# A new order for the first 28 slices of an attention-and-feed-forward kernel: eight PSUM banks for products before the first output tile, fewer fillers

## The chip, the core and the metric

The kernel runs on one core of a Trainium2 chip. The metric is the device time of one launch in microseconds (us), as the median of several executions. The kernel before takes about 224.4 us. The work is almost all on TensorE, so this is a case about the last half per cent: what a hand-laid or computed order of instructions can still win or lose in the first 57 us.

## The reference, cut to what matters

```python
def _attn_ref(x, state):                     # x: (8, 8, 512, 64), state: (8, 8, 32, 64)
    scores = scale * x @ state^T             # 512 x 32 for each batch and head
    a = softmax(scores);  xread = a @ state
    a2 = softmax(scale * state @ x^T);  sread = a2 @ x
    return concatenate([xread, sread], axis=2)

def reference(x, state, w_gate, w_val, w_out):
    y = attn(x, state) reshaped to (8*544, 512)
    return (relu(y @ w_gate) * (y @ w_val)) @ w_out      # 512 -> 1536 -> 512
```

Inputs and output are float32; the kernel computes in bf16 with float32 sums.

## The kernel before

For the x rows, the product `a @ state @ w` is reordered: first `U = state @ w` for each batch (small products, "c" and "u" units), then `a @ U` ("gv" slices of 128 of the 1536 columns, four matmuls of 128x512 each), then relu and multiply, then the output product ("o" parts). The state rows are read by small "sr" products. The kernel uses eight banks of PSUM, the memory that the products are written to, and names the bank of each tile by a number. The first 28 gv slices, with all preparation, are laid out by hand in a list of words; later slices are generated by a loop.

```python
    def bank(name, kind="r"):
        if given:
            n = given.pop(0)                 # the listed program: the number after @
        ...
        else:
            n = turn["r"] % 6 if kind == "r" else 6 + turn["o"] % 2      # the generated part
            turn[kind] += 1
        return psum.tile([128, 512], FP32, name=name, tag=f"b{n}")

    def u_mm(dst, b, w, lo, n):              # U units: 64x32 tiles of the array, in groups of eight
        for j in range(NJ):
            for parity in range(2):
                r = 64 * parity
                nc.tensor.matmul(dst[parity][32 * j:32 * j + 32], stT[r:r + 64, b, j, ...],
                                 wsb[r:r + 64, j, lo:lo + n], start=True, stop=True)

    def gv_mm(ps, b, jf, w, kc):             # full products, 128x128 weights, 512 columns
        nc.tensor.matmul(ps[w], U[b][:, w, kc, f0:f0 + 128], ANS[b][:, kc]..., ...)

    def sr_mm(b, kind="r"):                  # 32 small products into one bank
        ps = held["sr", b] = bank("sr_ps", kind)[:, 0:2 * DP]...
    def sr_norm(b):                          # VectorE reads that bank: reciprocal, then multiply
        nc.vector.reciprocal(out=rr, in_=ps[:, :, D])
        nc.vector.tensor_tensor(out=sn, in0=ps[:, :, 0:D], in1=rr..., op=ALU.mult)

    def spin(n, cols=512):                   # fillers: products on zeros, to keep the array busy
        for i in range(n):
            nc.tensor.matmul(warm_ps[:, 0:cols], warm[:, 0:128], warm[:, 0:cols], ...)

    program = """
    dx.1.0.2 ... spin.7 stT.0@0 xc.0.0.dve dw.0.0.128 sto.0.act ...
    [... some 240 words: loads (dw, dx), transposes (xT, aT), scores (sc), U units (c, u) and
         their copies (co, uo), slices (gv, re, mu), output parts (o) ...]
    gv.2.0@21 mu.1.8 re.2.0 o.0.7 mu.2.0 o.0.8 o.0.9@7 of.0.2.dve sr.1@3 sn.1 xp.2 xp.3
    """
    [... then a loop: gv, relu, mult for slices 28 to 107, with o parts and the next batches]
```

Read `c.1.512.256@54` as: U unit of batch 1, columns 512 to 767, in banks 5 and 4. `sr.1@3` is the sr product of batch 1 in bank 3.

The softmax here doesn't subtract the row's maximum and nothing guards it: scores larger than these inputs give would overflow.

Of the kernel before, what the change touches and what calls it, by code (L numbers as in the profile page):

```python
# [16 lines left out]
def kernel(  # L17
# [52 lines left out]
    stT = const.tile([128, B, NJ, 64], BF16, name="stT")  # L70
# [5 lines left out]
    xf, xb, xT, e_sn, a_sn, ANS, U, hsb, sr_sb = {}, {}, {}, {}, {}, {}, {}, {}, {}  # L76
# [362 lines left out]
             "c": c_unit, "co": c_out, "u": u_unit, "uo": u_out, "gv": gv, "re": relu, "mu": mult, "o": out_part,  # L439
             "of": fin_x, "xn": x_next, "xp": x_pad, "sr": sr_mm, "sn": sr_norm}  # L440
    program = """
    dx.1.0.2 dx.1.1.2 stc.0.0.act stc.0.1.dve spin.7 stT.0@0 xc.0.0.dve dw.0.0.128 sto.0.act dw.1.0.128 on xc.0.1.dve
    spin.3 xT.0.1@1 dw.0.128.128 xT.0.0@2 xo.0.1.dve xo.0.0.act dw.1.128.128 spin.3 sc.0.0@3 dw.0.256.256 ex.0.0
    spin.1 xT.0.2@4 xT.0.3@5 xo.0.2.dve dw.1.256.256 xo.0.3.act nr.0.0 spin.3 sc.0.1@0 dw.0.512.256 xT2.1.0@1 ex.0.1
    nx.0.0 xo2.1.0.act nr.0.1 dw.1.512.256 spin.2 xT2.1.1@2 xo2.1.1.act sc.1.0@3 dw.0.768.256 nx.0.1 ex.1.0
    dw.1.768.256 spin.2 c.1.0.128@45 c.0.0.128@01 co.1.0.128.0.dve aT.0.1@2 co.0.0.128.0.act aT.0.0@3 co.1.0.128.1.dve
    co.0.0.128.1.act dw.0.1024.256 sc.1.1@4 ao.0.1.dve ao.0.0.act nr.1.0 ex.1.1 dw.1.1024.256 spin.2 c.0.128.128@05
    gv.0.0@12 co.0.128.128.1.act nr.1.1 co.0.128.128.0.act nx.1.0.pool re.0.0 gv.0.1@34 mu.0.0 re.0.1 nx.1.1.pool
    c.1.128.128@50 mu.0.1 co.1.128.128.1.act c.0.256.256@12 co.1.128.128.0.act c.1.256.256@30 dw.0.1280.256
    co.0.256.256.0.dve co.0.256.256.1.act aT.1.1@5 aT.1.0@4 co.1.256.256.0.act co.1.256.256.1.dve dw.1.1280.256  # L450
    gv.0.3@21 ao.1.1.act ao.1.0.dve dx.2.0.1 re.0.3 gv.0.2@30 mu.0.3 ds re.0.2 c.1.512.256@54 mu.0.2 gv.1.2@21
    co.1.512.256.1.act co.1.512.256.0.act do.0.6 c.0.512.256@30 re.1.2 gv.1.5@45 co.0.512.256.0.dve xp.1
    co.0.512.256.1.act mu.1.2 re.1.5 gv.1.3@23 mu.1.5 re.1.3 gv.1.1@04 do.6.12 mu.1.3 re.1.1 c.1.768.256@15 xp.0
    mu.1.1 gv.1.4@23 co.1.768.256.0.act co.1.768.256.1.act c.0.768.256@04 re.1.4 gv.1.0@15 co.0.768.256.0.dve
    co.0.768.256.1.act df.3 mu.1.4 re.1.0 gv.1.6@20 mu.1.0 re.1.6 gv.0.4@41 mu.1.6 re.0.4 gv.0.6@35 mu.0.4 re.0.6
    gv.1.7@20 mu.0.6 re.1.7 c.0.1024.256@41 c.0.1280.256@35 mu.1.7 co.0.1024.256.0.act xT2.2.0@2 stc.1.0.pool
    co.0.1024.256.1.act co.0.1280.256.1.dve xT2.2.1@0 stc.1.1.pool co.0.1280.256.0.act xo2.2.0.dve gv.0.5@41
    stc.3.0.pool stc.3.1.pool xo2.2.1.dve re.0.5 stc.2.1.pool gv.0.10@53 stc.2.0.pool mu.0.5 re.0.10 stT.1@2 gv.0.9@40
    mu.0.10 sto.1.act re.0.9 sc.2.1@1 gv.0.8@52 ex.2.1 mu.0.9 re.0.8 nr.2.1 gv.0.11@34 re.0.11 mu.0.8 gv.0.7@10
    nx.2.1.pool mu.0.11 re.0.7 sc.2.0@5 o.0.0@6 mu.0.7 ex.2.0 nr.2.0 c.1.1280.256@32 c.1.1024.256@14  # L460
    co.1.1280.256.1.act u.2.1.1024@50 o.0.1 co.1.1024.256.0.dve co.1.1024.256.1.act nx.2.0.pool uo.2.1.1024.1.dve
    uo.2.1.1024.0.act o.0.2 co.1.1280.256.0.act u.2.0.0@21 xn.3 of.0.0.dve u.2.1.0@45 uo.2.0.0.1.act u.2.1.512@03
    uo.2.1.0.0.dve o.0.3@7 uo.2.1.0.1.act uo.2.0.0.0.dve uo.2.1.512.0.act aT.2.0@1 aT.2.1@4 uo.2.1.512.1.dve
    ao.2.0.act o.0.4 ao.2.1.act o.0.5 gv.2.1@50 of.0.1.act re.2.1 gv.1.10@23 mu.2.1 re.1.10 gv.1.11@14 mu.1.10 re.1.11
    gv.2.3@50 mu.1.11 re.2.3 gv.2.2@23 mu.2.3 re.2.2 u.2.0.1024@14 u.2.0.512@50 mu.2.2 uo.2.0.1024.1.act sr.0@2
    o.0.6@6 uo.2.0.512.1.act uo.2.0.512.0.dve sn.0 gv.1.9@34 uo.2.0.1024.0.dve re.1.9 gv.1.8@05 mu.1.9 re.1.8
    gv.2.0@21 mu.1.8 re.2.0 o.0.7 mu.2.0 o.0.8 o.0.9@7 of.0.2.dve sr.1@3 sn.1 xp.2 xp.3
    """
    for word in program.split():
        word, _, banks = word.partition("@")  # L470
# [107 lines left out]
```

## Time and profile before

| | before |
|---|---|
| time, median of 3 | 224.46 us (224.29 to 224.59) |
| execution that was profiled | 225.65 us, span on the core 223.9 us |
| TensorE (PE) busy | 96% of the span |
| first gv product | 14.43 us |
| first generated slice (slice 28) | 57.28 us |

The profiled execution is 1.2 us longer than the median of the timed ones.

In the views PE is TensorE, DVE is VectorE, ACT is ScalarE and POOL is GpSimd. The page of the profile, its lines for the span, for PE, and the rows of busy tenths for PE and the loads (40 slices of 5.6 us; 9 is 90% or more; the DMA row counts packet time over 16 engines; its 0 in the eighth place is 7%, with 24 GB/s moved there), and the chain that ended last, by engine:

```profile
span 223.9 us, 4840 instructions
...
PE 215.5 (96%) x1937; PEld 105.8 (47%) x1967; DVE 129.0 (58%) x226; ACT 124.8 (56%) x236; POOL 53.0 (24%) x58
...
PE   7899999999999999999999999999999999999994
...
DMA  7999999070146671781159114511311111111132
...
PE 84%; DMA 9%; POOL 4%; issue 2%; DVE 0%; POOLq 0%; DVEq 0%
```

PE is the limit. The loads are full from the second to the seventh slice, to 39 us, so the listed program meets the load queue there; no later slice reaches 90%.

The timeline of PE in the kernel before, 16.9 to 25 us (columns: start us, length us, engine, line, operation, out<-in, shape, count, and idle time before it if any):

```profile
16.86 0.30 PE L291 MATMUL upc<-wv_sb,stT 64*32 64x256 bf16 x8
...
17.44 0.62 PE L235 MATMUL aT_ps<-id,a_sn 128*128 128x128 bf16 x8
17.97 1.90 PE L316 MATMUL gv_ps<-ans,U 128*128 128x512 bf16 x7
19.80 0.30 PE L291 MATMUL upc<-wg_sb,stT 64*32 64x256 bf16 x8
19.92 0.29 PE L291 MATMUL upc<-wv_sb,stT 64*32 64x256 bf16 x8
20.15 1.04 PE L316 MATMUL gv_ps<-ans,U 128*128 128x512 bf16 x4
21.11 0.30 PE L291 MATMUL upc<-wg_sb,stT 64*32 64x256 bf16 x8
21.23 0.29 PE L291 MATMUL upc<-wv_sb,stT 64*32 64x256 bf16 x8
21.46 2.77 PE L316 MATMUL gv_ps<-ans,U 128*128 128x512 bf16 x11
24.15 0.30 PE L291 MATMUL upc<-wg_sb,stT 64*32 64x256 bf16 x8
24.27 0.29 PE L291 MATMUL upc<-wv_sb,stT 64*32 64x256 bf16 x8
24.50 1.04 PE L316 MATMUL gv_ps<-ans,U 128*128 128x512 bf16 x4
```

No idle time is printed, because a matmul's modelled end (0.38 us after its start) hides gaps shorter than that. The starts tell more. Four products of a gv slice start 0.216 us apart, so a slice is worth 0.86 us; but from 20.15 to 21.11 us, one slice, are 0.96 us, and a single unit between slices takes 0.35 us (19.80 to 20.15), although its second half starts 0.12 us after its first. So TensorE loses time in going from full products to 64x32 tiles and back. (Some matmul records are missing from a trace, hence counts like x7 and x11.)

And the end of the listed program in the kernel before, same columns:

```profile
55.10 1.89 PE L353 MATMUL o_ps<-wo_sb,h_sb 128*128 128x512 bf16 x8
56.92 0.43 PE L264 MATMUL sr_ps<-xa,e_sn 128*32 128x65 bf16 x32
57.28 1.04 PE L316 MATMUL gv_ps<-ans,U 128*128 128x512 bf16 x3
```

The slice at 57.28 us is the first generated one; the last of the 32 sr products starts at 57.16 us, so the gap between the two is 0.13 us.

### The profile page before, as it was taken

What the parts mean: (1) busy time and instruction counts of PE and PEld (TensorE: products, weight loads), DVE (VectorE), ACT (ScalarE), POOL (GpSimd) and SP (SyncE); (2) the same over time, 40 slices, a digit from 0 to 9 for tenths busy, and PEclk for the clock granted to TensorE, in tenths of its full rate; (3) what the DMA queues carried; (4) which work ended last, traced back from release to release, by engine and by line L of the source; (5) the groups of instructions that cost most, each with busy time, mean ns of one, the idle gap of its engine ahead of it and who ended that gap; (6) DMA issues with size and microseconds to landing.
All of it is one profiled execution on the core that took longest, in us unless ns stands there. A gap on an engine that the chain in (4) does not pass through costs nothing.

```text
span 223.9 us, 4840 instructions
## 1 busy us (share of the span) xinstructions
PE 215.5 (96%) x1937; PEld 105.8 (47%) x1967; DVE 129.0 (58%) x226; ACT 124.8 (56%) x236; POOL 53.0 (24%) x58
## 2 busy tenths in 40 slices
PE   7899999999999999999999999999999999999994
PEld 2544354444544444444444444444444445666543
DVE  3587888757595648663876468646874433222100
ACT  4599877865467644665557456545655444222221
POOL 8698828503302434006000700000000000000000
PEclk9999999999999999999999999999999999999999
DMA  7999999070146671781159114511311111111132
GB/s 157 176 195 197 215 225 278 24 187 3 47 106 225 112 267 47 160 265 50 50 118 276 49 60 99 107 50 47 94 50 47 48 47 50 48 64 74 54 94 94
DMA packets 37799, 25.48 MB, mean 114 GB/s; under 512 B 18864, under 2 KB 33200, under 8 KB 37776
## 3 DMA queue, kind: packets, MB, share of 16 engines
q1 hardware_dynamic: 24912, 16.85, 26.2%
q0 software_dynamic: 11968, 7.47, 21.5%
q10 hardware_dynamic: 896, 0.85, 1.4%
q8 instruction: 15, 0.25, 0.4%
q14 instruction: 8, 0.07, 0.1%
HBM read 18.35 MB, written 8.91 MB: 122 GB/s over the span
## 4 chain that ended last, share of the span: by engine, by line
PE 84%; DMA 9%; POOL 4%; issue 2%; DVE 0%; POOLq 0%; DVEq 0%
PE o_ps L353 38%; PE gv_ps L316 31%; DMA xb<-in_x_dram 9%; PE gv_ps L333 5%; PE up L291 4%; PE sr_ps L264 1%; POOL wv_sb L110 1%; PE sc_ps L200 1%; PE o_ps L379 1%; POOL wg_sb L110 1%; POOL a_sn L219 1%; PE xT_ps L186 0%; POOL xb L412 0%; PE stT_ps L129 0%; POOL xb L420 0%
## 5 line engine op out<-in xcount | busy, mean ns | idle before, releaser
L316 PE MATMUL gv_ps<-ans,U 128*128 128x512 bf16 x373 | 93.9, 380 | 0.5
L353 PE MATMUL o_ps<-wo_sb,h_sb 128*128 128x512 bf16 x357 | 91.6, 380 | 2.1 <-issue 1.9
L344 DVE TENSOR_TENSOR h_sb<-gv_ps,g_sb 128x512 bf16<-128x512 f32 x96 | 65.3, 689 | 44.2 <-ACT g_sb L340 43.3
L340 ACT ACTIVATE g_sb<-gv_ps 128x512 bf16<-128x512 f32 (+1 forms) x108 | 62.7, 580 | 49.3 <-PE gv_ps L316 34.5
L316 PEld LDWEIGHTS <-U 128*128 128x128 bf16 x384 | 35.8, 98 | 40.5 <-issue 0.6
L353 PEld LDWEIGHTS <-h_sb 128*128 128x128 bf16 x372 | 35.2, 98 | 39.9 <-issue 1.7
L361 ACT COPY o_sb<-o_ps 128x512 f32<-128x512 f32 x29 | 17.1, 590 | 16.5 <-PE o_ps L353 16.5
L301 ACT CAST U<-up 128x512 bf16<-128x512 f32 x36 | 18.9, 594 | 11.4 <-PE up L291 11.4
L301 DVE CAST U<-up 128x512 bf16<-128x512 f32 x36 | 22.8, 684 | 2.2 <-PE up L291 1.9
L142 POOL CAST xb<-xf 128x1024 bf16<-128x1024 f32 x10 | 10.1, 1040 | 53.6 <-DMA xf<-in_x_dram 32.6
L256 POOL COPY xa<-xb 128x2048 bf16<-128x2048 bf16 (+1 forms) x9 | 15.7, 1747 | 11.5 <-issue 6.6
L213 DVE TENSOR_REDUCE cs<-e_sn 128x16 f32<-128x512 bf16 x16 | 10.9, 683 | 7.7 <-ACT e_sn L207 7.7
L344 DVE TENSOR_TENSOR hs_sb<-gv_ps,g_sb 128x256 bf16<-128x256 f32 x12 | 5.1, 425 | 15.3 <-PE gv_ps L333 10.5
L207 ACT ACTIVATE e_sn<-sc_ps 128x512 bf16<-128x512 f32 x16 | 9.6, 600 | 5.6 <-PE sc_ps L200 5.5
L291 PEld LDWEIGHTS <-stT 64*32 64x32 bf16 x512 | 5.7, 90 | 11.2 <-issue 10.0
L311 ACT CAST U<-upc 128x512 bf16<-128x512 f32 (+1 forms) x20 | 9.6, 532 | 1.4 <-PE upc L291 1.3
L219 DVE TENSOR_TENSOR a_sn<-e_sn,rc 128x512 bf16<-128x512 bf16 x12 | 8.5, 709 | 0.6
L432 PE MATMUL warm_ps<-hs_sb 128*128 128x512 bf16 x20 | 7.2, 470 | 1.4 <-DVE hs_sb L396 1.2
L200 PEld LDWEIGHTS <-xT 128*128 128x128 bf16 x128 | 5.7, 98 | 3.8 <-ACT xT L177 0.7
L291 PE MATMUL up<-wg_sb,stT 64*32 64x512 bf16 x144 | 7.4, 383 | 0.0
L333 PE MATMUL gv_ps<-br,wg_sb 128*128 128x256 bf16 x48 | 7.2, 273 | 0.1
L333 PE MATMUL gv_ps<-br,wv_sb 128*128 128x256 bf16 x48 | 7.2, 273 | 0.0
(64 smaller groups left out, 129.5 us busy)
## 6 DMA issues: line engine op xcount, KB each, us to landing
out_dram<-o_sb SPq DMA_DIRECT2D x31, 256.0 KB, 2.3
xf<-in_x_dram SPq DMA_DIRECT2D x4, 1024.0 KB, 6.0
wo_sb<-in_moe_w_out_dram POOLq DMA_DIRECT2D x2, 768.0 KB, 15.4
wg_sb<-in_moe_w_gate_dram POOLq DMA_DIRECT2D x5, 256.0 KB, 8.7
wv_sb<-in_moe_w_val_dram POOLq DMA_DIRECT2D x5, 256.0 KB, 10.5
xf<-in_x_dram POOLq DMA_DIRECT2D x1, 1024.0 KB, 16.0
xb<-in_x_dram POOLq DMA_DIRECT2D x3, 256.0 KB, 7.1
xb<-in_x_dram POOLq DMA_DIRECT2D x1, 512.0 KB, 12.5
```

What stands on the lines that cost most here:

```text
L142: copy[eng](out=xb[b][:, :, hs].rearrange("p c h d -> p h c d"), in_=xf[b][:, hs])
L213: nc.vector.reduce_sum(out=cs, in_=e_v, axis=AX.X)
L219: {"dve": nc.vector, "pool": nc.gpsimd}[eng].tensor_tensor(out=by_pair(a_sn[b], jp).rearrange("p r (j n) -> p r j n", n=Ns), in0=e_v, in1= ...
L256: nc.gpsimd.tensor_copy(out=v[:, hs:hs + src.shape[1]], in_=src)
L291: nc.tensor.matmul(dst[parity][32 * j:32 * j + 32], stT[r:r + 64, b, j, 32 * parity:32 * parity + 32], wsb[r:r + 64, j, lo:lo + n], start= ...
L301: copy[eng](out=U[b][:, w, kc, lo:lo + 512], in_=held["u", b, w, lo][kc])
L316: nc.tensor.matmul(ps[w], U[b][:, w, kc, f0:f0 + 128], ANS[b][:, kc].rearrange("p c t -> p (c t)"), start=(kc == 0), stop=(kc == NK - 1))
L333: nc.tensor.matmul(ps[w][:, 0:nt], wsb[:, j, f0:f0 + 128], br[:, j].rearrange("p b n -> p (b n)"), start=(j == 0), stop=(j == NJ - 1))
L340: nc.scalar.activation(out=g_sb[:, 0:n], in_=ps[0][:, 0:n], func=AF.Relu)
L344: nc.vector.tensor_tensor(out=dst, in0=ps[1][:, 0:n], in1=held["g", b, jf][:, 0:n], op=ALU.mult)
L353: nc.tensor.matmul(held["o", b, tsub], src[:, jf, tsub * 128:(tsub + 1) * 128], wo_sb[:, jf], start=(jf == 0), stop=(jf == NF - 1))
L361: copy[eng](out=o_sb, in_=held["o", b, tsub])
```

## The change

The intent is to raise the use of TensorE in the first 28 slices: a new, computed order of the same work, in which banks 6 and 7 (later the output banks) hold products until the first output tile is begun, and 15 fillers instead of 23. Loads keep their order and sizes. The work between the first word and the first generated slice is the same. The diff replaces the whole list; its core:

```diff
-    dx.1.0.2 dx.1.1.2 stc.0.0.act stc.0.1.dve spin.7 stT.0@0 xc.0.0.dve dw.0.0.128 sto.0.act dw.1.0.128 on xc.0.1.dve
-    spin.3 xT.0.1@1 dw.0.128.128 xT.0.0@2 xo.0.1.dve xo.0.0.act dw.1.128.128 spin.3 sc.0.0@3 dw.0.256.256 ex.0.0
-    spin.1 xT.0.2@4 xT.0.3@5 xo.0.2.dve dw.1.256.256 xo.0.3.act nr.0.0 spin.3 sc.0.1@0 dw.0.512.256 xT2.1.0@1 ex.0.1
+    dx.1.0.2 dx.1.1.2 stc.0.0.act stc.0.1.dve xc.0.0.act dw.0.0.128 spin.6 stT.0@0 xT.0.0@1 xc.0.1.dve dw.1.0.128 on
+    sto.0.dve xT.0.1@2 xo.0.0.dve dw.0.128.128 xo.0.1.act dw.1.128.128 dw.0.256.256 spin.4 xT.0.3@3 dw.1.256.256
+    xT.0.2@4 xo.0.3.dve sc.0.0@5 xo.0.2.act ex.0.0 sc.0.1@6 dw.0.512.256 xT2.1.0@0 ex.0.1 nr.0.0 xo2.1.0.act
 [... cut ...]
-    gv.0.3@21 ao.1.1.act ao.1.0.dve dx.2.0.1 re.0.3 gv.0.2@30 mu.0.3 ds re.0.2 c.1.512.256@54 mu.0.2 gv.1.2@21
-    co.1.512.256.1.act co.1.512.256.0.act do.0.6 c.0.512.256@30 re.1.2 gv.1.5@45 co.0.512.256.0.dve xp.1
+    co.1.256.256.1.act mu.0.1 re.0.2 gv.1.0@46 mu.0.0 ds re.1.0 mu.0.2 c.1.512.256@20 c.0.512.256@37
+    co.1.512.256.0.act co.1.512.256.1.dve gv.1.1@14 co.0.512.256.1.act do.0.6 co.0.512.256.0.dve re.1.1 gv.1.4@52
 [... cut ...]
-    o.0.6@6 uo.2.0.512.1.act uo.2.0.512.0.dve sn.0 gv.1.9@34 uo.2.0.1024.0.dve re.1.9 gv.1.8@05 mu.1.9 re.1.8
-    gv.2.0@21 mu.1.8 re.2.0 o.0.7 mu.2.0 o.0.8 o.0.9@7 of.0.2.dve sr.1@3 sn.1 xp.2 xp.3
+    mu.2.0 gv.2.2@34 of.0.1.act re.2.2 gv.1.6@20 mu.2.2 re.1.6 o.0.6@6 mu.1.6 o.0.7 o.0.8 gv.2.1@15 of.0.2.dve re.2.1
+    gv.2.3@34 mu.2.1 re.2.3 o.0.9@7 mu.2.3 sr.0@2 sr.1@0 sn.0 sn.1 xp.2 xp.3
```

More of the change, by code (lines that the diff above doesn't have):

```diff
@@ L441 @@
     program = """
-    dx.1.0.2 dx.1.1.2 stc.0.0.act stc.0.1.dve spin.7 stT.0@0 xc.0.0.dve dw.0.0.128 sto.0.act dw.1.0.128 on xc.0.1.dve
-    spin.3 xT.0.1@1 dw.0.128.128 xT.0.0@2 xo.0.1.dve xo.0.0.act dw.1.128.128 spin.3 sc.0.0@3 dw.0.256.256 ex.0.0
-    spin.1 xT.0.2@4 xT.0.3@5 xo.0.2.dve dw.1.256.256 xo.0.3.act nr.0.0 spin.3 sc.0.1@0 dw.0.512.256 xT2.1.0@1 ex.0.1
-    nx.0.0 xo2.1.0.act nr.0.1 dw.1.512.256 spin.2 xT2.1.1@2 xo2.1.1.act sc.1.0@3 dw.0.768.256 nx.0.1 ex.1.0
-    dw.1.768.256 spin.2 c.1.0.128@45 c.0.0.128@01 co.1.0.128.0.dve aT.0.1@2 co.0.0.128.0.act aT.0.0@3 co.1.0.128.1.dve
@@ L447 @@
-    co.0.0.128.1.act dw.0.1024.256 sc.1.1@4 ao.0.1.dve ao.0.0.act nr.1.0 ex.1.1 dw.1.1024.256 spin.2 c.0.128.128@05
-    gv.0.0@12 co.0.128.128.1.act nr.1.1 co.0.128.128.0.act nx.1.0.pool re.0.0 gv.0.1@34 mu.0.0 re.0.1 nx.1.1.pool
-    c.1.128.128@50 mu.0.1 co.1.128.128.1.act c.0.256.256@12 co.1.128.128.0.act c.1.256.256@30 dw.0.1280.256
-    co.0.256.256.0.dve co.0.256.256.1.act aT.1.1@5 aT.1.0@4 co.1.256.256.0.act co.1.256.256.1.dve dw.1.1280.256
-    gv.0.3@21 ao.1.1.act ao.1.0.dve dx.2.0.1 re.0.3 gv.0.2@30 mu.0.3 ds re.0.2 c.1.512.256@54 mu.0.2 gv.1.2@21
@@ L452 @@
-    co.1.512.256.1.act co.1.512.256.0.act do.0.6 c.0.512.256@30 re.1.2 gv.1.5@45 co.0.512.256.0.dve xp.1
-    co.0.512.256.1.act mu.1.2 re.1.5 gv.1.3@23 mu.1.5 re.1.3 gv.1.1@04 do.6.12 mu.1.3 re.1.1 c.1.768.256@15 xp.0
-    mu.1.1 gv.1.4@23 co.1.768.256.0.act co.1.768.256.1.act c.0.768.256@04 re.1.4 gv.1.0@15 co.0.768.256.0.dve
-    co.0.768.256.1.act df.3 mu.1.4 re.1.0 gv.1.6@20 mu.1.0 re.1.6 gv.0.4@41 mu.1.6 re.0.4 gv.0.6@35 mu.0.4 re.0.6
-    gv.1.7@20 mu.0.6 re.1.7 c.0.1024.256@41 c.0.1280.256@35 mu.1.7 co.0.1024.256.0.act xT2.2.0@2 stc.1.0.pool
@@ L457 @@
-    co.0.1024.256.1.act co.0.1280.256.1.dve xT2.2.1@0 stc.1.1.pool co.0.1280.256.0.act xo2.2.0.dve gv.0.5@41
-    stc.3.0.pool stc.3.1.pool xo2.2.1.dve re.0.5 stc.2.1.pool gv.0.10@53 stc.2.0.pool mu.0.5 re.0.10 stT.1@2 gv.0.9@40
-    mu.0.10 sto.1.act re.0.9 sc.2.1@1 gv.0.8@52 ex.2.1 mu.0.9 re.0.8 nr.2.1 gv.0.11@34 re.0.11 mu.0.8 gv.0.7@10
-    nx.2.1.pool mu.0.11 re.0.7 sc.2.0@5 o.0.0@6 mu.0.7 ex.2.0 nr.2.0 c.1.1280.256@32 c.1.1024.256@14
-    co.1.1280.256.1.act u.2.1.1024@50 o.0.1 co.1.1024.256.0.dve co.1.1024.256.1.act nx.2.0.pool uo.2.1.1024.1.dve
@@ L462 @@
-    uo.2.1.1024.0.act o.0.2 co.1.1280.256.0.act u.2.0.0@21 xn.3 of.0.0.dve u.2.1.0@45 uo.2.0.0.1.act u.2.1.512@03
-    uo.2.1.0.0.dve o.0.3@7 uo.2.1.0.1.act uo.2.0.0.0.dve uo.2.1.512.0.act aT.2.0@1 aT.2.1@4 uo.2.1.512.1.dve
-    ao.2.0.act o.0.4 ao.2.1.act o.0.5 gv.2.1@50 of.0.1.act re.2.1 gv.1.10@23 mu.2.1 re.1.10 gv.1.11@14 mu.1.10 re.1.11
-    gv.2.3@50 mu.1.11 re.2.3 gv.2.2@23 mu.2.3 re.2.2 u.2.0.1024@14 u.2.0.512@50 mu.2.2 uo.2.0.1024.1.act sr.0@2
-    o.0.6@6 uo.2.0.512.1.act uo.2.0.512.0.dve sn.0 gv.1.9@34 uo.2.0.1024.0.dve re.1.9 gv.1.8@05 mu.1.9 re.1.8
@@ L467 @@
-    gv.2.0@21 mu.1.8 re.2.0 o.0.7 mu.2.0 o.0.8 o.0.9@7 of.0.2.dve sr.1@3 sn.1 xp.2 xp.3
+    dx.1.0.2 dx.1.1.2 stc.0.0.act stc.0.1.dve xc.0.0.act dw.0.0.128 spin.6 stT.0@0 xT.0.0@1 xc.0.1.dve dw.1.0.128 on
+    sto.0.dve xT.0.1@2 xo.0.0.dve dw.0.128.128 xo.0.1.act dw.1.128.128 dw.0.256.256 spin.4 xT.0.3@3 dw.1.256.256
+    xT.0.2@4 xo.0.3.dve sc.0.0@5 xo.0.2.act ex.0.0 sc.0.1@6 dw.0.512.256 xT2.1.0@0 ex.0.1 nr.0.0 xo2.1.0.act
+    dw.1.512.256 spin.2 xT2.1.1@1 nr.0.1 xo2.1.1.act sc.1.0@2 dw.0.768.256 nx.0.0 dw.1.768.256 ex.1.0 spin.2
@@ new lines @@
+    c.1.0.128@34 nx.0.1 sc.1.1@5 co.1.0.128.1.act c.0.0.128@60 co.1.0.128.0.dve dw.0.1024.256 aT.0.1@1 ex.1.1
+    co.0.0.128.0.dve aT.0.0@2 co.0.0.128.1.act ao.0.1.dve dw.1.1024.256 ao.0.0.act spin.1 c.1.128.128@43 nr.1.1
+    c.0.128.128@56 co.1.128.128.1.act gv.0.0@01 co.0.128.128.0.act nr.1.0 co.0.128.128.1.act dw.0.1280.256 re.0.0
+    gv.0.1@23 co.1.128.128.0.act nx.1.1 re.0.1 nx.1.0 dw.1.1280.256 c.0.256.256@57 c.1.256.256@60 co.0.256.256.1.act
+    co.0.256.256.0.dve aT.1.0@4 aT.1.1@2 co.1.256.256.0.act ao.1.0.dve gv.0.2@75 dx.2.0.1 ao.1.1.dve
@@ new lines @@
+    co.1.256.256.1.act mu.0.1 re.0.2 gv.1.0@46 mu.0.0 ds re.1.0 mu.0.2 c.1.512.256@20 c.0.512.256@37
+    co.1.512.256.0.act co.1.512.256.1.dve gv.1.1@14 co.0.512.256.1.act do.0.6 co.0.512.256.0.dve re.1.1 gv.1.4@52
+    mu.1.0 xp.0 re.1.4 gv.1.3@07 mu.1.1 re.1.3 mu.1.4 gv.0.5@31 mu.1.3 do.6.12 re.0.5 gv.0.3@65 mu.0.5 xp.1 re.0.3
+    c.0.768.256@40 c.0.1024.256@27 mu.0.3 co.0.768.256.1.act gv.1.2@31 co.0.1024.256.1.act co.0.768.256.0.dve df.3
+    re.1.2 gv.0.4@65 co.0.1024.256.0.dve re.0.4 mu.1.2 gv.1.5@07 mu.0.4 re.1.5 gv.0.9@43 mu.1.5 re.0.9 gv.0.8@26
@@ new lines @@
+    mu.0.9 re.0.8 c.1.1280.256@15 c.0.1280.256@07 mu.0.8 co.1.1280.256.1.act xT2.2.1@4 co.0.1280.256.1.act
+    co.1.1280.256.0.dve xT2.2.0@3 stc.1.0.pool co.0.1280.256.0.act c.1.768.256@26 xo2.2.1.dve stc.1.1.pool
+    c.1.1024.256@57 xo2.2.0.act stc.3.0.pool gv.1.10@10 co.1.768.256.0.dve stc.2.0.pool co.1.768.256.1.dve
+    co.1.1024.256.1.act stc.2.1.pool stT.1@4 gv.1.11@23 stc.3.1.pool re.1.10 sto.1.dve co.1.1024.256.0.act mu.1.10
+    gv.0.11@76 re.1.11 re.0.11 mu.1.11 gv.1.7@41 mu.0.11 re.1.7 gv.1.9@50 mu.1.7 re.1.9 sc.2.0@2 gv.0.7@73 mu.1.9
@@ new lines @@
+    ex.2.0 re.0.7 nr.2.0 gv.0.6@46 re.0.6 mu.0.7 gv.0.10@15 mu.0.6 re.0.10 u.2.0.0@20 u.2.1.512@74 nx.2.0
+    uo.2.0.0.1.act u.2.0.512@31 o.0.0@6 mu.0.10 uo.2.0.512.1.act uo.2.1.512.0.act uo.2.0.0.0.dve sc.2.1@0 o.0.1
+    uo.2.0.512.0.act xn.3 uo.2.1.512.1.dve ex.2.1 u.2.1.1024@15 nr.2.1 u.2.1.0@23 uo.2.1.1024.0.act u.2.0.1024@40
+    o.0.2 uo.2.1.0.1.act uo.2.0.1024.1.dve uo.2.1.0.0.act o.0.3@7 nx.2.1 of.0.0.dve aT.2.1@1 gv.1.8@30
+    uo.2.1.1024.1.dve ao.2.1.act re.1.8 uo.2.0.1024.0.dve aT.2.0@2 o.0.4 ao.2.0.dve mu.1.8 gv.2.0@15 re.2.0 o.0.5
```

## The prediction

> **What bounds the kernel now.** TensorE: the page has PE busy 96% of 223.9 us, and the chain of waits lies 84% on it. In the timeline, products of 128x512 start every 0.216 us almost unbroken from 14.43 us (first gv product). The change touches only the listed program, which ends near 52 us; only waits and fillers before that can be won.
>
> The start is bound by the load queue. Landings in the trace: rest of x[0] 8.20 us, x[1] 9.52 and 10.83, first weight columns 11.56/12.30, columns 1024 up 25.56, x[2] 30.91, w_out 35.63 and 39.51. The load share is full until 39 us, and loads keep order and bytes, so these times should hold within 1 us.
>
> **What the change does.**
> 1. Fillers 23 to 15: one cold (0.427 us) and seven warm (0.216), 1.9 us, but nearly all inside waits for loads. Worth about 0.
> 2. The first scores of batch 0 move behind its last transposes (which wait for 8.20 us): the first exponential goes from 7.43 to about 9.45 us. Two sums (0.71+0.29 us each) and two scalings (0.61) then run back to back on VectorE: a_sn[0] complete at 13.4 instead of 12.33 us, first gv at 14.9 instead of 14.43 us. Loss 0.5 us there.
> 3. Scaling of batch 1 goes from POOL (two in 2.05 us) to VectorE (0.61 each).
> 4. Banks 6 and 7 serve until the first output tile, and units of U columns are paired. Each return from a unit to full products costs about 0.2 us (19.95, 21.26, 24.30, 25.61 us); two or three fewer: 0.4 to 0.6 us. Bank waits after 18 us were few, so banks alone buy little.
> 5. Columns 1024 up are wanted near 25 us, landing at 25.56: a new wait of about 0.6 us eats that gain. The transposes of x[2] stood at 30.96 us, right behind their landing, with 14 gv slices ahead in both orders: no lead passes 31 us.
> 6. Then o tiles come later, clear of w_out's landing (0.2 us waited before), and switches are fewer: -0.3 us.
> 7. At the end both sr products come last, and sr.1 takes bank 0, which the first generated slice also takes: it waits until VectorE has normalised sr.1 (0.16+0.29 us plus latencies), about +0.45 us.
>
> Sum: +0.1 at 31 us, -0.3, +0.45: about +0.25 us.
>
> **Clock.** The Trainium skill, "TensorE: Matmul & The Clock Gate", Part 1, says the array starts at half clock and is released after about 3.4 us of sustained work. The trace agrees: fillers start every 0.427 us until 4.85 us, then 0.216. With fewer fillers TensorE idles from 3.7 to 4.3 us and is emptier until 8.2 us; a late release could cost 1 to 2 us, which I hold unlikely.
>
> **Prediction.** 224.7 us, 80% range 223.7 to 225.7. Faster by over 2%: 0.01; within 2%: 0.97; slower by over 2%: 0.02.
>
> **What would show it.** In the timeline: first exponential near 9.5 us, first gv near 14.9; a wait for weights near 25.6; transposes of x[2] at 31.0 again; a gap of about 0.7 us between the last sr product and the first generated gv; unchanged spacing after.
>
> **What would make it wrong.** Loads landing earlier, or waits on ACT or VectorE in 14 to 31 us that I took for hidden in before: a gain up to 1 us. Late release of the clock, or VectorE running full there: a loss up to 2 us.

## The result, and the profile after

The changed kernel took 225.09 us (median of 4 runs, 224.72 to 225.67) beside 224.4 us for the kernel before. The ratio is 1.0032, with a 95% interval of 1.0009 to 1.0055. All ratios here are the mean time of one kernel's fast runs over the mean of the other's fast runs of the same rounds, so they are not quite the ratio of the medians. A later repetition gave 0.9995 (0.9978 to 1.0011). So the direction of the result is not certain from times alone; the traces say more.

The page of the changed kernel, the same lines:

```profile
span 223.9 us, 4813 instructions
...
PE 212.9 (95%) x1930; PEld 105.7 (47%) x1959; DVE 131.3 (59%) x233; ACT 123.3 (55%) x233; POOL 48.8 (22%) x54
...
PE   6789999999899999999999999999999999999994
...
DMA  6999999162046671791159114511311111111132
...
PE 82%; DMA 12%; POOL 2%; issue 2%; DVE 1%; POOLq 0%; DVEq 0%
```

PE is busy 2.6 us less, which is mostly fillers gone, and the span is the same, as it would be if the fillers stood in waits.

The timeline of PE in the changed kernel, 16 to 24.8 us:

```profile
16.11 0.30 PE L291 MATMUL upc<-wg_sb,stT 64*32 64x256 bf16 x8
16.80 0.30 PE L291 MATMUL upc<-wv_sb,stT 64*32 64x256 bf16 x8 [0.38 <-DMA wv_sb<-in_moe_w_val_dram]
...
17.25 0.62 PE L235 MATMUL aT_ps<-id,a_sn 128*128 128x128 bf16 x8
17.91 1.90 PE L316 MATMUL gv_ps<-ans,U 128*128 128x512 bf16 x7
19.74 0.30 PE L291 MATMUL upc<-wg_sb,stT 64*32 64x256 bf16 x8
19.86 0.29 PE L291 MATMUL upc<-wv_sb,stT 64*32 64x256 bf16 x8
19.97 0.29 PE L291 MATMUL upc<-wg_sb,stT 64*32 64x256 bf16 x8
20.08 0.29 PE L291 MATMUL upc<-wv_sb,stT 64*32 64x256 bf16 x8
20.30 4.49 PE L316 MATMUL gv_ps<-ans,U 128*128 128x512 bf16 x19
```

Two units now stand together, 0.56 us from 19.74 to 20.30, and five slices follow without a break. And at 16.80 us PE waits for a load: the second weights of columns 256 to 511 landed at 16.76 us. In the kernel before, the same unit ran at 16.86 us, right after the landing at 16.82.

The end of the listed program in the changed kernel, PE and then VectorE (DVE):

```profile
55.92 0.70 PE L264 MATMUL sr_ps<-xa,e_sn 128*32 128x65 bf16 x64
57.37 1.04 PE L316 MATMUL gv_ps<-ans,U 128*128 128x512 bf16 x3 [0.75 <-DVE sn L273]
```

```profile
56.42 0.17 DVE L271 RECIPROCAL rr<-sr_ps 128x2 f32<-128x2 f32 x1 [0.37 <-PE sr_ps L264]
56.62 0.29 DVE L273 TENSOR_TENSOR sn<-sr_ps,rr 128x128 bf16<-128x128 f32 x1
56.83 0.16 DVE L271 RECIPROCAL rr<-sr_ps 128x2 f32<-128x2 f32 x1
57.02 0.29 DVE L273 TENSOR_TENSOR sn<-sr_ps,rr 128x128 bf16<-128x128 f32 x1
```

The last sr product starts at 56.43 us, and the first generated slice at 57.37 us: a gap of 0.94 us, 0.81 more than before. It waits until VectorE has read the bank of the second sr product, at 57.31 us.

### One table that explains the times

Five events cut the program into stretches. W is the landing of the second weights of columns 256 to 511. S is the first gv slice after the transposes of `a` for batch 1 (17.97 us in the kernel before). X is the first transpose of x[2]. G is the first generated slice. All are starts or landings in the traces, in us; the last column is the time of the profiled execution. The kernels below "after" are the experiments of the next section.

| kernel | W | W to S | S to X | X to G | G to end | G | time |
|---|---|---|---|---|---|---|---|
| before | 16.82 | 1.15 | 12.98 | 26.33 | 166.60 | 57.28 | 225.65 |
| after | 16.76 | 1.15 | 12.36 | 27.10 | 166.53 | 57.37 | 225.67 |
| before_again | 16.19 | 1.20 | 12.82 | 26.17 | 167.18 | 56.37 | 225.36 |
| after_sr_bank3 | 16.02 | 1.15 | 12.36 | 26.15 | 166.52 | 55.68 | 223.97 |
| after_scores_early | 15.93 | 1.15 | 12.36 | 27.08 | 166.51 | 56.52 | 224.83 |
| after_both | 15.71 | 1.15 | 12.36 | 26.18 | 166.52 | 55.40 | 223.72 |
| after_again | 16.30 | 1.15 | 12.36 | 27.03 | 166.49 | 56.85 | 225.14 |
| before_sr_bank0 | 16.12 | 1.15 | 12.82 | 26.86 | 166.58 | 56.95 | 225.34 |
| before_paired | 16.54 | 1.15 | 12.54 | 26.17 | 166.58 | 56.41 | 224.79 |
| after_bank3_fillers | 16.08 | 1.53 | 12.36 | 26.18 | 166.52 | 56.14 | 224.46 |
| before_pad_split | 16.41 | 1.42 | 12.82 | 26.17 | 166.57 | 56.82 | 225.17 |
| after_pad_split | 16.73 | 1.15 | 12.36 | 27.16 | 166.50 | 57.41 | 225.69 |
| after_sr_before_o | 16.14 | 1.15 | 12.81 | 26.46 | 166.49 | 56.56 | 224.86 |
| after_bank3_pad_split | 15.88 | 1.15 | 12.36 | 26.24 | 166.52 | 55.63 | 223.96 |

For one order of instructions most stretches hardly vary. (In the first row S to X is 12.98 us because x[2] landed only at 30.91 us, 0.05 us before X.) What varies from execution to execution is W, by 1.1 us, with the landings of the loads. The mean of W is 16.42 us in the five profiles of the old order and 16.17 in the nine of the new one. As much of a difference is already in the landing of the rest of x[0] (7.29 and 7.05 us), up to which both kernels issue the same loads at the same times, so these profiles don't show that the new order moves W. The change moves two stretches: S to X is 0.46 us shorter (12.82 to 12.36) and X to G is 0.9 us longer (26.17 to 27.03, 27.08, 27.10 or 27.16). With about 0.07 us less after G the sum is +0.3 to +0.5 us. The time of a profiled execution is G plus 168.3 to 168.4 us in every row but one.

One wait is hidden in X to G. Four transposes of the state (`stT.1`) need the rest of the state, which lands about 1 us after x[2], and then POOL's conversion of it. The chain that ended last in the changed kernel runs through this load, and in the kernel before it runs through x[2] (start us, length us, what). First the kernel before:

```profile
18.42 12.49 DMA xb<-in_x_dram
30.96 1.08 PE xT_ps L186 x32
```

And the changed kernel:

```profile
19.66 11.42 DMA st_f<-in_state_dram
31.18 1.84 POOL st_b L124 x2
```

In all nine profiles of the new order `stT.1` starts 1.98 or 1.99 us after this landing, and TensorE has waited 0.21 to 0.51 us for it (from the start of the product in front of it, less 0.216). From there to G are 23.49 or 23.50 us in the five profiles without the wait for bank 0, and 24.31 us in the four with it. So in the new order G follows the landing of the state, and the bank costs 0.82 us. In the old order only the first profile of before waits for the state (0.19 us; it landed at 31.92 us), and the other four pass without a wait. With this wait taken out, X to G is 25.94 or 25.95 us in the new order without the bank wait, and 26.17 us in the old one with `sr.1` in bank 3.

### The profile page after: what moved, and what is told of

The parts are those of the page before. It is cut to its first block, busy times and chain, and to the rows that moved or that the text cites. A ratio compares the mean times of both kernels' runs of the same rounds, so it can differ in the third digit from the quotient of the medians.

```text
span 223.9 us, 4813 instructions
## 1 busy us (share of the span) xinstructions
PE 212.9 (95%) x1930; PEld 105.7 (47%) x1959; DVE 131.3 (59%) x233; ACT 123.3 (55%) x233; POOL 48.8 (22%) x54
## 4 chain that ended last, share of the span: by engine, by line
PE 82%; DMA 12%; POOL 2%; issue 2%; DVE 1%; POOLq 0%; DVEq 0%
PE o_ps L353 38%; PE gv_ps L316 31%; DMA st_f<-in_state_dram 5%; PE gv_ps L333 5%; PE up L291 4%; DMA wv_sb<-in_moe_w_val_dram 4%; DMA xb<-in_x_dram 3%; PE sc_ps L200 1%; PE o_ps L379 1%; PE sr_ps L264 1%; POOL st_b L124 1%; POOL xb L412 0%; PE stT_ps L129 0%; POOL xb L420 0%; DVE sn L273 0%
## 5 line engine op out<-in xcount | busy, mean ns | idle before, releaser
L301 DVE CAST U<-up 128x512 bf16<-128x512 f32 x35 | 22.1, 683 | 2.3 <-PE up L291 1.9
L142 POOL CAST xb<-xf 128x1024 bf16<-128x1024 f32 x10 | 10.1, 1040 | 56.6 <-DMA xf<-in_x_dram 42.8
L219 DVE TENSOR_TENSOR a_sn<-e_sn,rc 128x512 bf16<-128x512 bf16 x16 | 11.2, 713 | 0.3
L311 ACT CAST U<-upc 128x512 bf16<-128x512 f32 (+1 forms) x18 | 8.7, 542 | 1.5 <-PE upc L291 1.5
L291 PE MATMUL up<-wv_sb,stT 64*32 64x512 bf16 x144 | 7.1, 380 | 0.0
```

What stands on the lines that cost most here:

```text
L142: copy[eng](out=xb[b][:, :, hs].rearrange("p c h d -> p h c d"), in_=xf[b][:, hs])
L219: {"dve": nc.vector, "pool": nc.gpsimd}[eng].tensor_tensor(out=by_pair(a_sn[b], jp).rearrange("p r (j n) -> p r j n", n=Ns), in0=e_v, in1= ...
L301: copy[eng](out=U[b][:, w, kc, lo:lo + 512], in_=held["u", b, w, lo][kc])
```

## The experiments

Twelve kernels ran, each in five rounds beside the kernel before, four to a chip. All gave correct results. The kernel before had medians of 225.05, 225.32 and 225.14 us on the three chips (224.57 to 225.85), so it is slower and more scattered there than the 224.4 us of the first comparison.

The theories at the start were these. Theory A: the loss is at the end, in the wait for the bank of the last sr product, and the start does not matter because a load absorbs it. Theory B: the loss is at the start, where the first gv product comes late, and it is carried to the end. Theory C: fewer fillers cost something through the clock.

### before_again: the kernel before, unchanged

Edit: none.

> The kernel before, unchanged, timed against itself: ratio 1.000 within 0.001 in every theory. Its profile says how far the load landings differ from run to run: the rest of x[0] landed at 8.20 us in the profile of before and at 7.51 us in that of after, though both kernels issue the same loads at the same times up to there. If this is chance, this profile may show either.

Measured: 225.18 us, ratio 1.0008 (0.9988 to 1.0028). The rest of x[0] landed at 6.46 us, where the first profile of before had 8.20 and the other twelve 6.53 to 7.70. So the profile on which the prediction was built was of an execution with unusually late loads. This second profile also shows something else: G to end is 167.18 us and not 166.6. See before_pad_split below.

### after_sr_bank3: the bank of the last sr product alone

```diff
-    gv.2.3@34 mu.2.1 re.2.3 o.0.9@7 mu.2.3 sr.0@2 sr.1@0 sn.0 sn.1 xp.2 xp.3
+    gv.2.3@34 mu.2.1 re.2.3 o.0.9@7 mu.2.3 sr.0@2 sr.1@3 sn.0 sn.1 xp.2 xp.3
```

> The changed kernel with its last sr product in bank 3 instead of bank 0. Theory A (end): the loss of the change is the wait of the first generated slice for the bank of sr.1, and a later start is absorbed where x[2] lands. Then this wins 0.55 us over the changed kernel: ratio to before about 1.0005, and the gap of 0.94 us between the last sr product and the first generated gv shrinks to about 0.15 us. Theory B (start): the loss is the first gv product 0.55 us later after the landing of x[0], carried to the end. Then the gap shrinks too, but the ratio stays near 1.003 only if something later gives the time back; a pure B expects 1.0025 to 1.0035. Theory C (fewer fillers, clock): ratio unchanged near 1.003.

Measured: 224.0 us, ratio 0.9960 (0.9940 to 0.9980). The end of the listed program in the timeline of PE:

```profile
55.04 0.70 PE L264 MATMUL sr_ps<-xa,e_sn 128*32 128x65 bf16 x64
55.68 1.04 PE L316 MATMUL gv_ps<-ans,U 128*128 128x512 bf16 x3
```

The gap is 0.12 us, as Theory A said, and X to G falls by 0.88 us, from 27.03 (after_again) to 26.15. One digit in the list turns the change from a loss into a gain. The ratio is lower than expected by 0.4%. The stretches explain about half of it: 0.46 us won in S to X and 0.07 after G are a ratio of 0.9976. The rest is not explained; the kernel before ran slower in these rounds than in the first comparison.

### after_scores_early: batch 0's first scores back in front

```diff
-    ... spin.4 xT.0.3@3 dw.1.256.256 xT.0.2@4 xo.0.3.dve sc.0.0@5 xo.0.2.act ex.0.0 sc.0.1@6
-    dw.0.512.256 xT2.1.0@0 ex.0.1 nr.0.0 xo2.1.0.act ... nr.0.1 xo2.1.1.act sc.1.0@2 dw.0.768.256 nx.0.0
+    ... spin.4 sc.0.0@5 ex.0.0 xT.0.3@3 dw.1.256.256 xT.0.2@4 xo.0.3.dve xo.0.2.act nr.0.0 nx.0.0 sc.0.1@6
+    dw.0.512.256 xT2.1.0@0 ex.0.1 xo2.1.0.act ... nr.0.1 xo2.1.1.act sc.1.0@2 dw.0.768.256
```

> The changed kernel with the first scores of batch 0, their exponential, sum and scaling put back ahead of the last transposes of batch 0. First gv product 0.5 us earlier, measured from the landing of the rest of x[0], in all theories. Theory A: no more than 0.2 us of it is left after x[2] lands: ratio 1.002 to 1.003. Theory B: ratio about 1.0005.

Measured: 225.27 us, ratio 1.0015 (0.9992 to 1.0039). The first exponential started at 6.64 us instead of 8.72 (after) or 8.59 (after_again), but the first gv product was not earlier against the loads: it came 3.80 us after the second half of x[1] landed, as in after (14.29 less 10.49) and after_again (3.81). This is a miss in all theories: the first gv product follows x[1], whose transposes and copies stand ahead of it in the instructions of PE and ACT, and not batch 0's scores. Theory B falls by the traces: the start gains nothing, and W to S is 1.15 us with either order. (The interval of the ratio alone would hold 1.0005.)

### after_both: both edits

Edit: the two diffs above.

> Both edits at once. Theory A: as with the bank alone, 1.000 to 1.0005. Theory B: as with the scores alone, 1.0005. If both losses are real and independent, about 0.998.

Measured: 224.45 us, ratio 0.9982 (0.9961 to 1.0004). The intervals of this kernel and of after_sr_bank3 overlap; the stretches are the same in both, 12.36 and 26.18 against 26.15 us. The scores add nothing to the bank.

### after_again: the changed kernel, once more

Edit: none.

> The changed kernel, unchanged, once more, to have it beside the others on one chip. Ratio to before 1.001 to 1.004: the first generated gv comes 0.4 us earlier through the middle of the program and 0.8 us later through the wait for bank 0.

Measured: 225.2 us, ratio 0.9995 (0.9978 to 1.0011): below the expected range. The stretches repeat those of the first profile of after (12.36, and 27.03 against 27.10). The kernel before took 225.32 us on this chip, with runs from 224.57 to 225.72. The three comparisons of the changed order with before (this one, the first one, and after_pad_split with its cut copies) give 1.0032, 0.9995 and 1.0017; their mean, 1.0015, is 0.33 us, near the 0.3 to 0.5 us of the traces.

### before_sr_bank0: the loss put into the kernel before

```diff
-    gv.2.0@21 mu.1.8 re.2.0 o.0.7 mu.2.0 o.0.8 o.0.9@7 of.0.2.dve sr.1@3 sn.1 xp.2 xp.3
+    gv.2.0@21 mu.1.8 re.2.0 o.0.7 mu.2.0 o.0.8 o.0.9@7 of.0.2.dve sr.1@0 sn.1 xp.2 xp.3
```

> The kernel before with only the bank of its last sr product changed, 3 to 0, so that the first generated slice must wait for it. Theory A (the loss lies in this bank): slower than before by 0.7 to 0.9 us, ratio 1.003 to 1.004, and the gap between the last sr product and the first generated gv goes from 0.12 to 0.8 to 1.0 us. Rival (the gap merely shows time lost or won earlier): ratio 1.000.

Measured: 225.34 us, ratio 1.0012 (0.9991 to 1.0033). The end in the timeline of PE:

```profile
55.90 0.43 PE L264 MATMUL sr_ps<-xa,e_sn 128*32 128x65 bf16 x32
56.95 0.61 PE L316 MATMUL gv_ps<-ans,U 128*128 128x512 bf16 x2 [0.62 <-DVE sn L273]
```

The gap goes from 0.13 to 0.81 us, and X to G from 26.17 to 26.86 us, 0.69 more, in the other order of instructions as well. The times alone don't settle it: the interval holds both 1.000 and 1.003. With one sr product in front of the slice the wait is shorter than in the changed kernel, where VectorE has two to normalise.

### before_paired: two U units moved to their neighbours, in banks 6 and 7

```diff
-    ... c.1.512.256@54 mu.0.2 gv.1.2@21 co.1.512.256.1.act co.1.512.256.0.act do.0.6 c.0.512.256@30 re.1.2 ...
-    ... c.1.768.256@15 xp.0 mu.1.1 gv.1.4@23 co.1.768.256.0.act co.1.768.256.1.act c.0.768.256@04 re.1.4 ...
+    ... c.1.512.256@54 c.0.512.256@67 mu.0.2 gv.1.2@21 co.1.512.256.1.act co.1.512.256.0.act do.0.6 re.1.2 ...
+    ... c.1.768.256@15 c.0.768.256@67 xp.0 mu.1.1 gv.1.4@23 co.1.768.256.0.act co.1.768.256.1.act re.1.4 ...
```

> The kernel before with two of its single U units moved next to their neighbours (columns 512 and 768 of batch 0 right behind those of batch 1), in banks 6 and 7, which are free until the first output tile. Theory D: the win of the new order in 14 to 30 us is two returns fewer from U units to full products, 0.19 us each: first gv to the transposes of x[2] 0.4 us shorter, ratio to before 0.998. Rival: the win comes from fewer bank waits or fewer fillers; then this stretch is unchanged and the ratio 1.000.

Measured: 224.53 us, ratio 0.9968 (0.9951 to 0.9984). S to X is 12.54 us against 12.82: 0.28 us of the 0.46 that the changed kernel wins there, and less than the expected 0.4. In this trace one gv product after the first pair came 0.18 us late, which would make up the difference. It starts at 21.14 us, 0.06 us after ScalarE's copies of the pair's first unit end (21.08 us), and it takes that unit's two banks (`gv.1.5@45` after `c.1.512.256@54`): a bank wait, as far as the trace shows; no run tested it. The ratio is 0.7 us, more than twice what the trace shows, and the rest is not explained. What stands is that pairing units, in banks that were free, shortens exactly this stretch.

### after_bank3_fillers: all 23 fillers back

```diff
-    spin.6 stT.0@0 xT.0.0@1 ...  ex.0.0 sc.0.1@6 ...  ao.0.0.act spin.1 ...  sr.0@2 sr.1@0 sn.0 sn.1
+    spin.7 stT.0@0 spin.3 xT.0.0@1 ...  ex.0.0 spin.3 sc.0.1@6 ...  ao.0.0.act spin.2 ...  sr.0@2 sr.1@3 sn.0 sn.1
```

> The changed kernel with the last sr product in bank 3, and all 23 fillers of the kernel before put back, nearly all where TensorE waits. Theory: fillers are worth nothing: same as with the bank alone, ratio 0.996 to 0.997. Rival (fewer fillers bring the win): ratio about 0.998 to 1.000.

Measured: 224.27 us, ratio 0.9951 (0.9934 to 0.9969), against 0.9960 with 15 fillers on another chip. In the times, fillers are worth nothing within 0.2%, which is 0.4 us. Theory C falls: more fillers did not bring the clock earlier either. The full clock came at 7.19 us in this profile, the latest of all fourteen. The profile is not free of a cost: the transposes of the rest of x[0] start behind the fillers at 7.90 us, 0.49 us after the landing (0.05 us in after), and W to S is 0.38 us longer. Whether the late clock or the fillers themselves did this is not shown.

### before_pad_split and after_pad_split: a chance event, and what it isn't

The profile of before_again was 0.6 us longer after G. TensorE falls behind by 0.58 us between 88.8 and 90.6 us (beside before_paired). The VectorE and POOL timelines show an event just before, first VectorE:

```profile
83.01 2.29 DVE L219 TENSOR_TENSOR a_sn<-e_sn,rc 128x512 bf16<-128x512 bf16 x1
85.23 1.28 DVE L344 TENSOR_TENSOR h_sb<-gv_ps,g_sb 128x512 bf16<-128x512 f32 x2
```

And POOL in the same profile:

```profile
82.87 1.90 POOL L256 COPY xa<-xb 128x2048 bf16<-128x2048 bf16 x1
```

The scaling took 2.29 us instead of 0.69; it stood behind a POOL copy that had begun 0.14 us earlier. In the first profile of before the scaling began before the copy: it took 0.91 us, and the copy 2.24 instead of 1.90. The Trainium skill, "SBUF — State Buffer", section "SBUF: two separate sides", says that VectorE operations with two SBUF inputs and GpSimd operations that read SBUF share a port pair as an exclusive lock: the one that starts first holds it for its whole instruction, and the other fully blocks. These numbers agree with it, and so do the others: in all fourteen profiles this scaling starts while a POOL instruction runs, the copy in before_again alone and the conversion of x (L142) in the other thirteen. In twelve it ends 0.54 us after that instruction does, whatever its own length (0.71 to 2.29 us); in the last two it takes its usual 0.69 us. The rival was that this event makes the scatter of the kernel before. The edit, in both kernels:

```diff
-            nc.gpsimd.tensor_copy(out=v[:, hs:hs + src.shape[1]], in_=src)
+            n = 2 if b > 3 else src.shape[1]
+            for k in range(0, src.shape[1], n):
+                nc.gpsimd.tensor_copy(out=v[:, hs + k:hs + k + n], in_=src[:, k:k + n])
```

> The kernel before, with the padded copies of x for batches 4 to 7 on POOL cut into four pieces each. In one of two profiles of the kernel before, VectorE's scaling at 83.0 us took 2.29 us instead of 0.69, next to a POOL copy of 1.90 us that had begun at 82.8, and the rest of the program ran 0.6 us later. Theory E: VectorE and POOL wait for each other, POOL's copy must end first, and this chance event makes some executions of before 0.6 us longer. With pieces of about 0.5 us the scaling near 83 us stays under 1.3 us, the time from the first generated gv to the end is 166.5 us, the executions scatter less, and the ratio to before is 0.9975 to 0.9995. Rival: the event has another cause; then ratio 1.000 and the same scatter.

Measured: 225.09 us, ratio 1.0000 (0.9988 to 1.0013). The longest scaling near 83 us was 1.26 us and G to end 166.57 us, as expected, but the time is no better and the scatter is the same (224.53 to 225.17). So the event is real in one profile, and it isn't the main cause of the scatter.

> The changed kernel with the same cut. It showed no scaling over 1.22 us in its two profiles, so little should change: ratio to before 0.998 to 1.002, and 0.4 to 0.6 us over the kernel before with the same cut (ratio of the two 1.002 to 1.003), which is the change without the chance event.

Measured: 225.15 us, ratio 1.0017 (0.9998 to 1.0036), and 1.0017 over before_pad_split as well, from the two ratios. That is 0.38 us, a little below the expected range of 1.002 to 1.003, and what the stretches of the table add up to.

### after_sr_before_o: bank 0 kept, the wait hidden

```diff
-    gv.2.3@34 mu.2.1 re.2.3 o.0.9@7 mu.2.3 sr.0@2 sr.1@0 sn.0 sn.1 xp.2 xp.3
+    gv.2.3@34 mu.2.1 re.2.3 sr.0@2 sr.1@0 sn.0 sn.1 o.0.9@7 mu.2.3 xp.2 xp.3
```

> The changed kernel with both sr products and their normalising moved ahead of the last output part, bank 0 kept. If the loss is the wait and not the bank itself, the 0.86 us of the output part hide it: the first generated gv follows without the gap of 0.94 us, and the kernel gains 0.6 to 0.8 us over the changed one, ratio to before 0.996 to 0.9975. Rival (bank 0 is slow in itself, or the gap shows time lost earlier): no gain.

Measured: 224.52 us, ratio 0.9981 (0.9968 to 0.9994), a little above the expected range, and 0.36% under after_pad_split on the same chip. X to G is 26.46 us: 0.6 us less than in the changed kernel, with the same bank. With the wait for the state taken out (0.51 us here) it is 25.95 us against 26.76, so the whole loss is hidden. It is the wait and not the bank. The end in the timeline of PE:

```profile
55.05 0.71 PE L264 MATMUL sr_ps<-xa,e_sn 128*32 128x65 bf16 x64
55.69 1.04 PE L353 MATMUL o_ps<-wo_sb,h_sb 128*128 128x512 bf16 x4
56.56 1.03 PE L316 MATMUL gv_ps<-ans,U 128*128 128x512 bf16 x4
```

This profile also shows the one case in the new order in which late loads ruled S to X, 12.81 instead of 12.36 us. PE in its timeline, 24 to 30.2 us:

```profile
24.34 0.29 PE L291 MATMUL upc<-wg_sb,stT 64*32 64x256 bf16 x8
24.77 0.30 PE L291 MATMUL upc<-wv_sb,stT 64*32 64x256 bf16 x8
...
30.11 1.08 PE L186 MATMUL xT_ps<-id,xb 128*64 128x128 bf16 x32
```

Without a wait the second line starts 0.11 us after the first; here it starts 0.43 us after it, because the weights of columns 1024 up landed at 24.73 us. The transposes follow x[2], which landed at 30.06 us. The lead from pairing was lost to the loads there.

### after_bank3_pad_split: the best candidate

Edit: the bank (`sr.1@3`) and the cut copies.

> The best candidate: the changed kernel with sr.1 in bank 3 and the pad copies cut. Ratio to before 0.995 to 0.9965, like the bank alone, scatter no larger.

Measured: 224.26 us, ratio 0.9974 (0.9959 to 0.9990), short of the expected range, with stretches of 12.36 and 26.24 us. The four kernels with the new order and bank 3 lie at 0.9951, 0.9960, 0.9974 and 0.9982. The new order with one digit changed is the version that beats both kernels: the kernel before by 0.2 to 0.5% (the interval of the smallest, after_both, reaches 1.0004), and the changed order by 0.3 to 0.4% on each of the three chips (after_both against after_scores_early, after_bank3_fillers against after_again, this one against after_pad_split).

## Why the prediction was right or wrong

The forecast of 224.7 us, in a range of 223.7 to 225.7, held: 225.09 us, within 2%, and a little slower. Its sum, +0.25 us, is near the +0.3 to +0.5 us of the traces. But the terms were less good than the sum, and errors cancelled: too little gain was seen before 31 us, too much after it, and too small a loss at the end. That the sum came so near is partly luck. The prediction also put the end of the listed program near 52 us, where it is 57.28 us; no term rests on it.

1. Fillers worth about 0: right. PE was busy 2.6 us less at the same span, and with all 23 back after_bank3_fillers was no slower in the times. Its profile does show a longer W to S (0.38 us), whose cause is open.
2. "First gv at 14.9 instead of 14.43 us. Loss 0.5 us there": wrong. The chain of batch 0's scores is not what the first gv product waits for. It comes 3.80 us after the second half of x[1] lands, with the scores early or late. And whatever happens there is then absorbed at W, the landing of weights for columns 256 up: S followed W by 1.15 us in eleven of fourteen profiles, in both orders. The step overlooked that wait in the profile of before, where it hid under the modelled ends of the matmuls.
3. Scaling of batch 1 on VectorE instead of POOL: right, 1.22 us for two in the changed kernel instead of 2.05, and no effect on S either.
4. The gain from pairing, 0.4 to 0.6 us: right in size and place. Between 17.4 and 31 us the kernel before goes from 64x32 tiles back to larger ones five times and the changed one three times; S to X falls by 0.46 us, 0.23 us for each block. The Trainium skill, "TensorEngine Tiling (Array Packing)", section "Tiling Modes", Key Properties, says that changing the tiling mode drains TensorE; the starts agree, though they don't show the drain itself. That more banks by themselves buy little is consistent with before_paired, which used banks 6 and 7 to pair; banks without pairing were not tried.
5. "A new wait of about 0.6 us eats that gain" and "no lead passes 31 us": the wait is wrong as stated, and the second claim is half right. In the nine profiles of the new order the weights of columns 1024 up landed at 23.6 to 24.8 us, not at 25.56. Only one of them (after_sr_before_o) shows the wait, of about 0.3 us, and a wait of about 0.1 us for x[2] behind it. Yet a lead does end at a load near 31 us, at one that the prediction listed no landing for: the rest of the state, for which all nine profiles of the new order wait. In the first profile of before, `stT.1` already waited for that landing, so in an execution like it no lead passes. In the three other profiles of the old order without pairing `stT.1` started 0.41 to 0.77 us later than this load alone would have allowed, and that much could be won. The mechanism is real; the landing times were taken from one execution, which was a slow one by 1.2 us, and treated as fixed "within 1 us", though that is larger than every effect under study.
6. "-0.3 us" after 31 us from fewer switches and later o tiles: wrong in the sum. X to G without the bank wait is 26.15 to 26.24 us in the new order (26.46 in after_sr_before_o) and 26.17 us in the old one (26.33 in the first profile). Nothing was won there. The step that failed is a wait that was not counted: the new order waits 0.21 to 0.51 us for the rest of the state and POOL's conversion of it. Without this wait it would need 0.22 us less than the old order, near the forecast; whether switches or o tiles bring that was not tested. In the first profile of after there is also a wait of 0.2 us for VectorE's copy of the transposes.
7. The wait for bank 0: right in mechanism, and shown by four kernels (after_sr_bank3, after_both, before_sr_bank0, after_sr_before_o). The term was mis-sized: +0.45 us was put down, +0.82 us came (0.94 less 0.12). The gap itself was put at 0.7 us. VectorE has to normalise both products, one after the other (56.42 to 57.31 us), and the hand-over without a wait is 0.12 us, not the 0.25 us that the forecast took off.

The clock: the prediction held a late release unlikely. Twelve profiles have it at 4.24 to 5.91 us, with no cost to be seen, and two at 6.85 and 7.19 us (before_pad_split, after_bank3_fillers; both have 23 fillers). In those two, W to S is 1.42 and 1.53 us instead of 1.15. That is about 0.3 us, but no experiment moved the clock alone, so the link is not shown.

Left open: why the executions of one kernel scatter by up to 1.6 us in these rounds. In the profiles the landings of the loads go with most of it (in the new order G follows the landing of the state), but what moves the loads was not found.

## What to carry to other kernels

When a kernel has several PSUM banks in rotation, look at the seam where a listed part hands over to a generated one: the last user of a bank there is the first thing the next part waits for, and one bank number cost more than a whole reordering won. Group products of the same array tiling; each block of small tiles between full products costs about 0.23 us here. A lead is worth something only up to the next load that it must wait for, so list every load behind it. And before arguing with fractions of a microsecond from one profile, check that the profiled execution's time is near the median, and take load landings from more than one.

## What the Trainium skill lacked or had wrong

- "TensorEngine Tiling (Array Packing)", Key Properties: says that a mode switch drains, with no figure. Here a block of 64x32 products between full ones cost 0.23 us beyond its own products ((12.82 - 12.36) / 2).
- "TensorE: Matmul & The Clock Gate", Part 1: puts the release around 4 us into sustained matmul activity, within 500 ns from run to run, and says further down that one kernel had 6, 11 or 14 slow matmuls. In the fourteen profiles here it lay between 4.24 and 7.19 us from the start of the program, which is 3.1 to 6.0 us after the first filler at 1.17 or 1.18 us, and 23 fillers did not bring it earlier than 15. TensorE has gaps in that time, so this does not show the page wrong; it shows that 500 ns is too narrow for such a start.
- "SBUF — State Buffer", "SBUF: two separate sides": right on the lock between VectorE and GpSimd; this case adds its size in a tuned kernel: a scaling of 2.29 us instead of 0.69 behind a copy of 1.90 us, and a copy of 2.24 us when the scaling began before it.
- No page gives the scatter of load landings between executions, as far as a search shows. Here the same load of weights, at the same place in the same queue, landed between 15.71 and 16.82 us, and this alone is larger than the effect under study.
